# Attention with a two-layer MLP: one chunk's second product is carried from block 1 into block 2

## The chip, the cores and the metric

The kernel runs on one core of a Trainium2 chip. It is one launch, and its time is the device time of that launch in microseconds (us); lower is better. Five instruction streams run side by side on the core: TensorE (PE: matrix products, with the loads of their stationary operand shown as PEld), VectorE (DVE), ScalarE (ACT), GpSimd (POOL), and SyncE (SP), which here only issues transfers. Each takes its instructions in the order in which the program lists them, and they meet at semaphores.

## The reference

Two things are computed one after the other: a linear attention over 8 batches and 8 heads (576 tokens, 64 features per head), and an MLP on the 4608 x 512 result.

```python
q_s = softmax(q, axis=-1)            # over the 64 features of a head
k_s = softmax(k, axis=2)             # over the 576 tokens
kv  = einsum('bhsd,bhse->bhde', k_s, v)
x   = einsum('bhsd,bhde->bhse', q_s, kv)   # then tokens x (heads * 64): 4608 x 512
h   = x @ w_in                       # 512 -> 2048
g   = h * clip(h + 3.0, 0.0, 6.0) / 6.0
out = g @ w_out                      # 2048 -> 512
```

All of it is float32; the weights arrive as float64 words and are decoded in the kernel.

## The kernel before, in words

**Blocks and chunks.** The 4608 tokens are cut into nine blocks of 512 (`j` = 0 to 8), and the 2048 hidden features into 16 chunks of 128 (`f`). For a block and a chunk there is a first product (x with a chunk of `w_in`, into the PSUM tile `ph`), the activation (ACT `L572` and DVE `L573`, giving `g`), a cut of `g` into a coarse and a fine part (`split`: a CAST on ACT at `L123`, a subtraction on DVE at `L124`), and a second product, which adds into four PSUM tiles `po`, one per 128 tokens. Each float32 product is made of three passes (coarse with coarse, coarse with fine, fine with coarse), so a chunk's second product is 12 matmuls of 128x512.

**Two ways of making the first product.** Blocks 0 and 1 use `gemm1`: 12 matmuls of 128x512 for a chunk. From block 2 on, `fast_pair` makes the first product of two chunks at once from seven products of half size (six matmuls of 128x256 each), out of sums of the weights that `fast_weights` has written to DRAM and `fetch` reads back. These seven products go into the tiles x and y (both named `ph`, two buffers) and z (`pz`), and each x has to be copied out by ACT (`L524`, `L530`, `L534`, `L540`) before the next may overwrite it. Between the products stand four gaps, `fill(4)`, `fill(7)`, `fill(7)`, `fill(6)`: so many matmuls of second products that wait in the list `pend` are put there, 24 in all, which is what two chunks have.

**The list `pend`.** `work(j, fs, gs)` is a generator of a chunk's (or a pair's) second-product matmuls; behind the last of a block it calls `store`. In blocks 0 and 1 each iteration makes the first product of chunk `f`, runs what stands in `pend` beyond a limit (`fill_one`), and appends chunk `f`. `store` (lines 596 to 607) scales the four `po` tiles into `ob` tiles, with ACT (`L606`) for tiles 0 and 2 and DVE (`L604`) for tiles 1 and 3, and sends each to DRAM (`L607`). The pool of `ob` has two buffers, taken in turn, and `fast_weights` takes two tiles from the same pool (`s12`, `s34`, `L464`) for sums of weights (`L466` to `L470`), which it then splits (`L468`, `L471`). The four `po` of the next block take the PSUM banks of the four before.

**Order.** From block 1 on the matmuls keep the order in which the code issues them (`keep_in_program_order`); the instructions of the other engines are put in order by a scheduler that works with estimated times and priorities. The attention of a later block (softmax of q and k, `kv`, `px`) is stepped along in between by `slot`, and `fast_weights(7)`, the last pair of weights, is made in the fourth slot of block 2's first pair (line 709).

Of the kernel before, what the change touches and what calls it, by code (L numbers as in the profile page):

```python
# [30 lines left out]
def attention_moe(  # L31
# [33 lines left out]
    NFC = w.shape[0]  # L65
# [60 lines left out]
    def load_w(f, sides=(0, 1)):  # L126
        if f not in raws:
            raws[f] = place(f, U32, f"raw{f}")
        a, b = 2 * DM * sides[0], 2 * DM * (sides[-1] + 1)
        nc.sync.dma_start(  # L130
            raws[f][:, a:b], w[f].rearrange("p s n -> p (s n)")[:, a:b]
        )
# [3 lines left out]
    def decode(f):  # L136

        n = 2 * DM
        pairs = raws.pop(f).rearrange("p (n two) -> p n two", two=2)
        low, high = pairs[:, :, 0], pairs[:, :, 1]
        v = moe.tile([P, n], F32, name="v", bufs=3)
        m = v
        nc.scalar.activation(m, high.bitcast(F32), AF.Abs)  # L148
        nc.vector.tensor_scalar(m, m, W_MIN, W_MAX, op0=ALU.max, op1=ALU.min)
        m = m.bitcast(U32)  # L150
        nc.vector.tensor_scalar(
            m, m, 3, 0x3FFFFFFF, op0=ALU.logical_shift_left, op1=ALU.bitwise_and
        )
        vu = v.bitcast(U32)
        nc.vector.scalar_tensor_tensor(
            vu, high, 0xC0000000, m, op0=ALU.bitwise_and, op1=ALU.bitwise_or
        )
        nc.scalar.activation(low, low, AF.Copy, scale=2.0**-29)
        nc.vector.tensor_tensor(vu, vu, low, op=ALU.add)
        parts = place(f, F32R, f"w_{f}").rearrange("p (s i n) -> p s i n", s=2, i=2)  # L160
        vs = v.rearrange("p (s n) -> p s n", s=2)
        if f not in BY_DMA:
            split(parts[:, :, 0], parts[:, :, 1], vs)
        else:

            hi, lo = parts[:, :, 0], parts[:, :, 1]
            nc.scalar.copy(hi, vs)
            nc.scalar.mul(lo, vs, -1.0)
            nc.gpsimd.dma_start(lo.bitcast(F32), vs, accum_op=ALU.add)
        wi[f], wo[f] = parts[:, 0], parts[:, 1]  # L170
# [280 lines left out]
    def fast_weights(pair):  # L451

        a, b = wi[2 * pair], wi[2 * pair + 1]
        kept[pair] = d = dr.tile([P, 7, 2, HT], F32, name=f"wf{pair}")
        for n, src in ((A11, a[:, :, 0:HT]), (A12, a[:, :, HT:]), (A22, b[:, :, HT:])):
            nc.sync.dma_start(d[:, n], src.bitcast(F32))
        whole = moe.tile([P, 2 * DM], F32, name="m", tag="v", bufs=3)
        for at, src in ((0, a), (TB, b)):
            nc.vector.tensor_add(
                whole[:, at : at + TB], src[:, 0].bitcast(F32), src[:, 1].bitcast(F32)  # L460
            )
        a11, a12, a21, a22 = (whole[:, n * HT : (n + 1) * HT] for n in range(4))
        hi, lo = (t.rearrange("p e n -> p (e n)") for t in (a, b))
        s12, s34 = (moe.tile([P, DM], F32, name="ob", bufs=2) for _ in range(2))  # L464
        s1, s2, s3, s4 = (t[:, n : n + HT] for t in (s12, s34) for n in (0, HT))
        nc.vector.tensor_add(s1, a21, a22)  # L466
        nc.vector.tensor_sub(s2, s1, a11)
        split(hi[:, 0:TB], lo[:, 0:TB], s12)  # L468
        nc.vector.tensor_sub(s3, a11, a21)
        nc.vector.tensor_sub(s4, a12, s2)  # L470
        split(hi[:, TB:], lo[:, TB:], s34)  # L471
        for e, t in enumerate((hi, lo)):
            nc.sync.dma_start(
                d[:, S1 : S4 + 1, e], t.bitcast(F32).rearrange("p (k n) -> p k n", k=4)
            )
# [10 lines left out]
    def fetch(count):  # L486
        for _ in range(count):
            key = next(wanted, None)
            if key is None:
                return  # L490
            j, pair, n = key
            f, h = RING[next(turn) % len(RING)]
            t = wi[f].rearrange("p a n -> p (a n)")[:, h * TB : (h + 1) * TB]
            t = t.rearrange("p (e n) -> p e n", e=2)
            nc.sync.dma_start(t.bitcast(F32), kept[pair][:, ORDER[n][0]])
            come[key] = t
# [65 lines left out]
    def gemm1(j, f):  # L562
        x_hi, x_lo = x_tiles[j]
        ph = ps_h.tile([P, TB], F32, name="ph", tag="ph")
        for cc in range(NCC):
            first, last = cc == 0, cc == NCC - 1
            w_hi, w_lo = (wi[f][:, i, cc * P : (cc + 1) * P] for i in (0, 1))
            mm(ph, w_hi, x_hi[:, cc, :], first, False)
            mm(ph, w_hi, x_lo[:, cc, :], False, False)
            mm(ph, w_lo, x_hi[:, cc, :], False, last)  # L570
        g = moe.tile([P, TB], F32, name="g", bufs=2)
        nc.scalar.activation(g, ph, AF.Relu, bias=three, scale=1.0)  # L572
        nc.vector.scalar_tensor_tensor(g, g, 6.0, ph, op0=ALU.min, op1=ALU.mult)  # L573
        g_hi = moe.tile([P, TB], F32R, name="g_hi", bufs=3)
        g_lo = moe.tile([P, TB], F32R, name="g_lo", bufs=3)
        split(g_hi, g_lo, g)
        return g_hi, g_lo
# [72 lines left out]
    pend = []  # L650
# [6 lines left out]
    def work(j, fs, gs):  # L657

        for f, g in zip(fs, gs):
            for fn, x in gemm2(f, *g, acc(j)):  # L660
                yield fn, x
            if f == NFC - 1:
                store(j, acc(j))
# [10 lines left out]
    def fill_one():  # L674
        for fn, x in pend.pop(0):
            fn(*x)

    for j in range(FAST):
        for f in range(NFC):
            if j == 0:  # L680
                if f + AHEAD < NFC:
                    load_w(f + AHEAD)
            elif not in_order:
                in_order.append(True)
            g = gemm1(j, f)
            if j == 0:
                if f + 2 < NFC:
                    decode(f + 2)
            elif f % 2:
                if f < 15:  # L690
                    fast_weights(f // 2)
                if f >= 7:
                    fetch(1 if f < 15 else 12 - len(come))
            next(step, None)

            while len(pend) > 1 - j:
                fill_one()
            pend.append(work(j, [f], [g]))
    for j in range(FAST, NB):
# [74 lines left out]
```

## Time and profile before

| | |
|---|---|
| median of 3 runs | 886.73 us (885.42 to 887.73) |
| the profiled execution | 889.86 us, span 888.1 us |
| TensorE | busy 855.5 us, 96% of the span |
| VectorE, ScalarE, GpSimd | 616.0, 462.9 and 131.4 us |
| granted TensorE clock, mean | 0.994 |

The span is the profiled stretch from the first to the last instruction; the execution's time has some 1.8 us more around it. A row of the timeline names start and length in us, the engine, the line, the operation, output and inputs, and in brackets how long the engine had been idle and what released it. Nearly all rows of TensorE name line 91, the helper `mm`; they are told apart by their tiles. Block 2's first pair begins at 240.98 us.

### The profile page before, as it was taken

The numbers are of one execution on the slowest core, as the hardware profiler recorded it, in microseconds if no ns is written. First come the engines' busy times: TensorE is split into PE (matmuls) and PEld (weight loads), VectorE is DVE, ScalarE is ACT, GpSimd is POOL, SyncE is SP. The second block draws the span as 40 slices with busy tenths as digits, with TensorE's granted clock in tenths as the row PEclk, the third lists the DMA queues.
The fourth block names the chain that finished last, engine by engine and source line by source line (L and its number), as shares of the span: only waits on it lengthen the run. The fifth ranks groups of instructions, "written<-read, shape, count | busy, mean of one in ns | idle before, by whom it ended". The sixth has DMA issues, their size and how long they took to land.

```text
span 888.1 us, 15250 instructions
## 1 busy us (share of the span) xinstructions
PE 855.5 (96%) x5380; PEld 735.9 (83%) x5380; DVE 616.0 (69%) x1267; ACT 462.9 (52%) x943; POOL 131.4 (15%) x328
## 2 busy tenths in 40 slices
PE   4799999999999999999999999999999999999998
PEld 3477777887788888888888888888888988898896
DVE  7999997899687766767675757675867665434333
ACT  7999644455355454545454545444545554434333
POOL 5000021122112211212020203020212120100000
PEclk9899999999999999999999999999999999999999
DMA  9994653638496767676777677676855575557541
GB/s 368 413 374 136 153 145 109 201 120 275 139 295 203 219 206 244 209 229 199 246 226 221 199 230 248 217 220 188 265 160 175 168 223 169 169 184 214 170 140 47
DMA packets 98202, 184.66 MB, mean 208 GB/s; under 512 B 9808, under 2 KB 24144, under 8 KB 96080
## 3 DMA queue, kind: packets, MB, share of 16 engines
q1 hardware_dynamic: 96192, 180.03, 63.1%
q0 software_dynamic: 1360, 2.62, 1.7%
q10 hardware_dynamic: 576, 1.05, 0.3%
q8 instruction: 43, 0.70, 0.3%
q14 instruction: 31, 0.25, 0.1%
HBM read 156.93 MB, written 24.12 MB: 204 GB/s over the span
## 4 chain that ended last, share of the span: by engine, by line
PE 78%; DMA 5%; DVE 3%; ACT 3%; issue 1%; POOL 0%; SPq 0%; ACTq 0%; POOLq 0%
PE po L91 38%; PE ph L91 30%; PE pz L91 4%; PE px L91 2%; PE pkv L91 2%; DMA qt<-in_qf_dram 2%; DMA out_dram<-ob 1%; DMA w<-v 1%; DMA kt<-in_kT_dram 1%; ACT w L123 0%; DVE w L124 0%; POOL swap L289 0%; PE pm L97 0%; ACT v L434 0%; ACT v L148 0%
## 5 line engine op out<-in xcount | busy, mean ns | idle before, releaser
L91 PE MATMUL po<-w,w 128*128 128x512 f32 x1008 | 261.2, 394 | 2.0 <-ACT w L123 1.9
L91 PEld LDWEIGHTS po<-w,w 128*128 128x128 f32 x1008 | 178.8, 189 | 32.0 <-ACT w L123 2.6
L91 PE MATMUL ph<-x_lo,w 128*128 128x256 f32 (+1 forms) x800 | 151.8, 304 | 1.5 <-DVE x_lo L124 0.6
L91 PEld LDWEIGHTS ph<-w,w 128*128 128x128 f32 x1008 | 134.4, 191 | 11.2 <-DVE second L535 1.6
L91 PE MATMUL ph<-w,w 128*128 128x256 f32 x1008 | 141.1, 285 | 1.4 <-DVE second L535 1.4
L91 PE MATMUL ph<-x_hi,w 128*128 128x256 f32 (+1 forms) x592 | 137.4, 335 | 1.9 <-DVE g L573 1.2
L91 PEld LDWEIGHTS ph<-x_lo,w 128*128 128x128 f32 x800 | 116.3, 189 | 16.5 <-DVE x_lo L124 1.4
L91 PEld LDWEIGHTS ph<-x_hi,w 128*128 128x128 f32 x592 | 92.2, 189 | 16.4 <-DVE x_lo L124 1.8
L124 DVE TENSOR_TENSOR w<-g,w 128x512 fp32r<-128x512 f32 x112 | 77.3, 690 | 36.9 <-ACT w L123 36.9
L123 ACT CAST w<-g 128x512 fp32r<-128x512 f32 x112 | 69.4, 619 | 60.7 <-DVE g L541 37.5
L91 PE MATMUL po<-w 128*128 128x512 f32 x336 | 86.7, 394 | 0.1
L91 PE MATMUL po<-w,g_hi 128*128 128x512 f32 x256 | 67.4, 400 | 1.1 <-ACT g_hi L123 1.1
L91 PEld LDWEIGHTS po<-w 128*128 128x128 f32 x336 | 59.4, 188 | 10.8 <-ACT w L123 0.5
L556 ACT ACTIVATE g<-second,three 128x512 f32<-128x512 f32 x56 | 40.5, 723 | 32.6 <-DVE second L554 26.1
L91 PEld LDWEIGHTS po<-w,g_hi 128*128 128x128 f32 x256 | 46.8, 188 | 11.8 <-ACT g_hi L123 1.6
L540 ACT ACTIVATE g<-ph,three 128x256 f32<-128x256 f32 x56 | 26.6, 474 | 57.2 <-PE ph L91 57.2
L541 DVE SCALAR_TENSOR_TENSOR g<-g,ph 128x256 f32<-128x256 f32 x56 | 23.2, 414 | 47.0 <-ACT g L540 46.8
L534 ACT COPY second<-ph 128x256 f32<-128x256 f32 x56 | 20.8, 372 | 61.9 <-PE ph L91 61.9
L557 DVE SCALAR_TENSOR_TENSOR g<-g,second 128x512 f32<-128x512 f32 x56 | 39.1, 698 | 15.3 <-ACT g L556 15.2
L535 DVE TENSOR_TENSOR second<-second,ph 128x256 f32<-128x256 f32 x56 | 23.2, 414 | 37.3 <-ACT second L534 37.3
L91 PE MATMUL pz<-x_hi,w 128*128 128x256 f32 x336 | 48.9, 281 | 0.0
L289 POOL COPY swap<-qr 32x16 f32<-32x16 f32 x112 | 30.9, 275 | 101.7 <-DVE qr L301 95.1
(125 smaller groups left out, 1258.5 us busy)
## 6 DMA issues: line engine op xcount, KB each, us to landing
w<-wf SPq DMA_DIRECT2D x392, 256.0 KB, 3.2
raw<-in_w_dram SPq DMA_DIRECT2D x16, 1024.0 KB, 13.4
out_dram<-ob SPq DMA_DIRECT2D x36, 256.0 KB, 3.3
vt<-in_v_dram SPq DMA_DIRECT2D x28, 325.0 KB, 3.6
wf<-w SPq DMA_DIRECT2D x16, 512.0 KB, 4.5
kt<-in_kT_dram SPq DMA_DIRECT2D x28, 288.0 KB, 3.0
ke<-in_k_dram SPq DMA_DIRECT2D x24, 320.0 KB, 3.1
qt<-in_qf_dram SPq DMA_DIRECT2D x28, 256.0 KB, 3.3
```

What stands on the lines that cost most here:

```text
L91: nc.tensor.matmul(out, lhsT, rhs, start=start, stop=stop, skip_group_check=goes_on)
L123: nc.scalar.copy(hi, src)
L124: engine.tensor_sub(lo, src, hi.bitcast(F32))
L289: nc.gpsimd.tensor_copy(swap[r : r + QD], stat[o : o + QD])
L534: nc.scalar.copy(second[:, HT:], x)
L535: nc.vector.tensor_add(second[:, HT:], second[:, HT:], y)
L540: nc.scalar.activation(r[:, HT:], x, AF.Relu, bias=three, scale=1.0)
L541: nc.vector.scalar_tensor_tensor(r[:, HT:], r[:, HT:], 6.0, x, op0=ALU.min, op1=ALU.mult)
L556: nc.scalar.activation(r, second, AF.Relu, bias=three, scale=1.0)
L557: nc.vector.scalar_tensor_tensor(r, r, 6.0, second, op0=ALU.min, op1=ALU.mult)
```

## The change

One condition, in the loop over blocks 0 and 1:

```diff
@@ -693,7 +693,7 @@
                     fetch(1 if f < 15 else 12 - len(come))
             next(step, None)
 
-            while len(pend) > 1 - j:
+            while len(pend) > (j == 0 or f == NFC - 1):
                 fill_one()
             pend.append(work(j, [f], [g]))
     for j in range(FAST, NB):
```

In block 0 the limit stays 1, in block 1 it stays 0 but for the last chunk, where it is now 1. So at `f` = 15 of block 1 the second product of chunk 14 is not run; it stays in `pend`, and chunk 15 is appended behind it. Block 2's first pair then has 24 matmuls for its four gaps where it had 12.

**TensorE, where block 1 ends and block 2 begins.** `w_1068` is the place of chunk 14's weights, `w_1135` that of chunk 15's; `pz` and `ph` are products of block 2's first pair. Before:

```order
L91 MATMUL pkv<-vt,ke 64x65 x10
L91 MATMUL po<-w_1068,g_hi 128x512 x8
L91 MATMUL po<-w_1068,g_lo 128x512 x4
L91 MATMUL pz<-x_hi_310,w_588 128x256 x6
L91 MATMUL ph<-x_hi_310,w_588 128x256 x6
L91 MATMUL po<-w_1135,g_hi 128x512 x2
L91 MATMUL po<-w_1135,g_lo 128x512
L91 MATMUL po<-w_1135,g_hi 128x512
L91 MATMUL ph<-w_333,w_657 128x256 x6
L91 MATMUL ph<-w_305,w_657 128x256 x6
L91 MATMUL po<-w_1135,g_hi 128x512
L91 MATMUL po<-w_1135,g_lo 128x512
```

Now:

```order
L91 MATMUL pkv<-vt,ke 64x65 x10
L91 MATMUL pz<-x_hi_310,w_588 128x256 x6
L91 MATMUL ph<-x_hi_310,w_588 128x256 x6
L91 MATMUL po<-w_1068,g_hi 128x512 x4
L91 MATMUL ph<-w_333,w_657 128x256 x6
L91 MATMUL ph<-w_305,w_657 128x256 x6
L91 MATMUL po<-w_1068,g_hi 128x512 x4
L91 MATMUL po<-w_1068,g_lo 128x512 x3
L91 MATMUL px<-qT_hi,kv_hi_0_1445 128x192
L91 MATMUL px<-qT_lo,kv_hi_0_1445 128x192
L91 MATMUL px<-qT_hi,kv_lo_0_1446 128x192
L91 MATMUL px<-qT_hi,kv_hi_0_2311 128x320
```

The 12 matmuls of chunk 14 have left the place ahead of the pair's first product, and the gaps behind the second and the fourth product are filled with them: 4, then 7, with the twelfth and six of chunk 15's in the third gap and chunk 15's last six in the fourth.

**VectorE, the first pair of block 2 and what follows.** With 24 matmuls in `pend` the generator calls `store` only at the `fill()` behind the pair, so it now comes behind `fast_weights(7)` in the code, and its `ob` tiles follow `s12` and `s34` in the pool. Before (`ob_2398` and `ob_2404` take `po` tiles 1 and 3 of block 1, `ob_2463` is `s12`):

```order
L546 SCALAR_TENSOR_TENSOR g_2414<-g_2414,first_2330 128x256
L604 TENSOR_SCALAR ob_2398<-po_1394 128x512
L307 STREAM_TRANSPOSE m_2454<-qt_2427 128x512
L459 TENSOR_TENSOR m_2460<-w_14_1068 128x512
L459 TENSOR_TENSOR m_2460<-w_15_1135 128x512
L604 TENSOR_SCALAR ob_2404<-po_1396 128x512
L124 TENSOR_TENSOR x_hi1_539<-v_2381,x_hi1_539 128x256
L535 TENSOR_TENSOR second_2331<-second_2331,ph_2328 128x256
L124 TENSOR_TENSOR qT_lo_2544<-m_2454,qT_hi_2543 128x512
L466 TENSOR_TENSOR ob_2463<-m_2460 128x256
```

Now there is no `L604` among these; behind `L297` on `qm_3002`, the maximum of the query tile `qt_2996`, come (`ob_2451` is `s12`, `ob_2452` is `s34`, `w_14_1068` and `w_15_1135` take their coarse and fine parts):

```order
L541 SCALAR_TENSOR_TENSOR g_2396<-g_2396,ph_2315 128x256
L467 TENSOR_TENSOR ob_2451<-ob_2451,m_2448 128x256
L124 TENSOR_TENSOR x_lo1_540<-v_2671,x_lo1_540 128x256
L554 TENSOR_TENSOR second_2319<-second_2319,ph_2316 128x256
L470 TENSOR_TENSOR ob_2452<-m_2448,ob_2451 128x256
L290 TENSOR_TENSOR qm_3002<-qm_3002,swap_3005 128x16
L124 TENSOR_TENSOR w_12_958<-g_2396,w_12_958 128x512
L124 TENSOR_TENSOR w_15_1135<-ob_2451,w_14_1068 128x512
L307 STREAM_TRANSPOSE m_2757<-qt_2730 128x512
L299 TENSOR_TENSOR qt_2996<-qt_2996,qm_3002 128x512
L557 SCALAR_TENSOR_TENSOR g_2471<-g_2471,second_2319 128x512
L527 TENSOR_TENSOR first_2491<-first_2491,pz_2490 128x256
```

and directly behind them:

```order
L124 TENSOR_TENSOR w_15_1135<-ob_2452,w_14_1068 128x512
L301 TENSOR_REDUCE qr_3003<-qt_2996 128x16
L124 TENSOR_TENSOR w_13_1017<-g_2471,w_13_1017 128x512
L604 TENSOR_SCALAR ob_2479<-po_1394 128x512
L546 SCALAR_TENSOR_TENSOR g_2570<-g_2570,first_2491 128x256
L297 TENSOR_REDUCE qm_3282<-qt_3276 128x16
L290 TENSOR_TENSOR qr_3003<-qr_3003,swap_3014 128x16
L303 TENSOR_SCALAR qr_3003<-qr_3003 128x16
L304 RECIPROCAL qr_3003<-qr_3003 128x16
L305 TENSOR_TENSOR qt_2996<-qt_2996,qr_3003 128x512
L290 TENSOR_TENSOR qm_3282<-qm_3282,swap_3285 128x16
L604 TENSOR_SCALAR ob_2485<-po_1396 128x512
```

`L604` for `po` tile 1 (`ob_2479`) now stands behind the whole work on the sums of weights, and waits for the last reading of `s34`, whose buffer it takes; `L604` for tile 3 (`ob_2485`) comes eight instructions later and waits until the transfer out of `ob_2479` has ended.

**ScalarE, the same stretch.** Before, both `L606` came ahead of the copy `L434` of `px`, in the first pair:

```order
L123 CAST kv_hi3_0_2311<-kv_2309 128x128
L524 COPY first_2330<-ph_2327 128x256
L606 ACTIVATE ob_2395<-po_1393 128x512
L545 ACTIVATE g_2414<-first_2330,three_90 128x256
L530 COPY second_2331<-ph_2327 128x256
L606 ACTIVATE ob_2401<-po_1395 128x512
L434 COPY v_2381<-px_2374 128x512
```

Now:

```order
L123 CAST w_14_1068<-ob_2452 128x512
L606 ACTIVATE ob_2476<-po_1393 128x512
L300 ACTIVATE qt_2996<-qt_2996 128x512
L123 CAST w_13_1017<-g_2471 128x512
L545 ACTIVATE g_2570<-first_2491,three_90 128x256
L606 ACTIVATE ob_2482<-po_1395 128x512
L300 ACTIVATE qt_3276<-qt_3276 128x512
L530 COPY second_2492<-ph_2488 128x256
L534 COPY second_2492<-ph_2488 128x256
```

`L606` for tile 0 (`ob_2476`) stands behind the cut of `s34`, `L606` for tile 2 (`ob_2482`) behind `L545` of the second pair, and the copies `L530` and `L534` of the second pair come behind `L300` on `qt_3276`, which on VectorE follows `L604` of `ob_2485`. On SyncE the four `L607` now stand among the two writes of the sums of weights (`L473`), and the read of `qt_2996` (`L328`) still follows the fetch (`L495`) that the pair's fifth product releases.

## The prediction

> **What bounds the kernel now.** The page comes first, for its spans, busy shares and the engine shares of the chain of work that ended last.
>
> ```profile
> span 888.1 us, 15250 instructions
> PE 855.5 (96%) x5380; PEld 735.9 (83%) x5380; DVE 616.0 (69%) x1267; ACT 462.9 (52%) x943; POOL 131.4 (15%) x328
> PE 78%; DMA 5%; DVE 3%; ACT 3%; issue 1%; POOL 0%; SPq 0%; ACTq 0%; POOLq 0%
> ```
>
> TensorE is busy 96% of the span and carries 78% of the chain. What the change can win is therefore idle time of TensorE in block 2's first pair, and what it can lose is new idle time there. The timeline of TensorE over the block boundary shows the first:
>
> ```profile
> 237.21 0.95 PE L91 MATMUL pkv<-vt,ke 128*64 128x65 f32 x20
> 238.09 2.13 PE L91 MATMUL po<-w,g_hi 128*128 128x512 f32 x8
> 240.98 0.87 PE L91 MATMUL pz<-x_hi,w 128*128 128x256 f32 x6
> 241.69 0.88 PE L91 MATMUL ph<-x_hi,w 128*128 128x256 f32 x6
> ...
> 246.40 0.25 PE L91 MATMUL px<-qT_hi,kv_hi 128*128 128x192 f32 x1
> ...
> 247.17 0.87 PE L91 MATMUL ph<-x_lo,w 128*128 128x256 f32 x6
> 248.72 0.98 PE L91 MATMUL ph<-x_lo,w 128*128 128x256 f32 x6 [0.44 <-ACT second L534]
> 251.13 0.98 PE L91 MATMUL ph<-w,w 128*128 128x256 f32 x6 [1.43 <-DVE second L535]
> ...
> 253.37 1.09 PE L91 MATMUL po<-w,w 128*128 128x512 f32 x4
> 254.30 1.59 PE L91 MATMUL ph<-w,w 128*128 128x256 f32 x12
> 255.73 1.78 PE L91 MATMUL po<-w,w 128*128 128x512 f32 x7
> 257.35 0.27 PE L97 MATMUL pm<-ident,kb 128*128 128x128 f32 x1
> 257.38 0.97 PE L91 MATMUL ph<-x_lo,w 128*128 128x256 f32 x6
> ```
>
> Two waits, 0.44 and 1.43 us, stand where the third and fourth gap have one matmul and none: the copies of `second` and its sum with y are waited for in the open. Starts, not lengths, give what a matmul costs, since neighbours overlap: six of 128x256 take 0.71 us (240.98 to 241.69), a 128x512 one 0.233 (253.37 to 254.30 for four), the six `px` 0.77 (246.40 to 247.17).
>
> Who is busy behind this? In the 12 us that follow, VectorE is. The table by stretches (columns: stretch, length, then busy us of PE, PEld, DVE, ACT, POOL with counts, granted clock, DMA share, GB/s) and six rows of its timeline:
>
> ```profile
> 252.00:264.00 12.00, 12.00 (x91) 10.52 (x91) 11.40 (x27) 6.77 (x14) 2.98 (x12) 1.00 0.94 307
> 256.31 0.41 DVE L527 TENSOR_TENSOR first<-first,pz 128x256 f32<-128x256 f32 x1
> 256.64 0.69 DVE L124 TENSOR_TENSOR w<-ob,w 128x512 fp32r<-128x512 f32 x1
> 257.24 0.71 DVE L307 STREAM_TRANSPOSE m<-qt 128x512 f32<-128x512 f32 x1
> 257.87 0.72 DVE L299 TENSOR_TENSOR qt<-qt,qm 128x512 f32<-128x512 f32 x1
> 258.51 0.68 DVE L124 TENSOR_TENSOR w<-ob,w 128x512 fp32r<-128x512 f32 x1
> 259.12 0.68 DVE L124 TENSOR_TENSOR w<-g,w 128x512 fp32r<-128x512 f32 x1
> ```
>
> 11.40 of 12 us: a full queue, in which an instruction of 128x512 delays the next by 0.62 us (256.64 to 259.12 for four) and one of 128x256 by 0.33 (256.31 to 256.64).
>
> **The change, part by part. What it wins.** Both orders agree up to 238.09 us. From there the new one puts the products first: `pz` 238.09, product 2 238.80, four `po` 239.51, two products 240.44, seven `po` 241.86, `px` 243.49, product 5 244.26, seven `po` 244.97, product 6 246.60, six `po` 247.31, product 7 248.71, then the second pair's `pz` 249.42 and product 250.13. Its first gap of `po` would start at 250.84, where the trace has 253.37: 2.53 us won, the two waits and the restarts around them. The second product of chunk 14 no longer covers chunk 15's activation, but the four `po` in the first gap need chunk 14's `g` alone, which was ready for 238.09, and the copies of x have seven, seven and six `po` over them (1.6, 1.6 and 1.4 us) against the 0.9 us from a product's start to its copy plus 0.37.
>
> **What it moves: `store`.** The first gap of the second pair needs `po` tiles 0 and 1 empty. Before, they were emptied inside the first pair. Now `L606` and `L604` follow the sums of weights, whose buffers they take. So I walk VectorE's new queue. Its first outside wait is `L297` on the query tile `qt_2996`, whose transfer SyncE issues right behind a fetch that product 5 releases:
>
> ```profile
> 248.07 0.33 SPq L495 DMA_DIRECT2D w<-wf  x1
> 248.49 0.49 SPq L328 DMA_DIRECT2D qt<-in_qf_dram  x1
> qt<-in_qf_dram SPq DMA_DIRECT2D x1, 256.0 KB, 3.6
> qt<-in_qf_dram SPq DMA_DIRECT2D x28, 256.0 KB, 3.3
> ```
>
> The last two rows are the landing of this very transfer and the median of all 28. The fetch went 0.90 us after product 5 began (247.17 to 248.07), the query tile 0.42 later: now 244.26 + 0.90 + 0.42 = 245.58. I take 3.3 us, because fewer transfers stand beside it than at 248.49: it lands at 248.88.
>
> From there the list in the order is nine instructions of 128x512 size up to `L604` of tile 1 (`L297`, `w_12`, `w_15`, `L307`, `L299`, `L557`, `w_15`, `L301`, `w_13`), six of 128x256 and a small one of 0.08: 9 x 0.62 + 6 x 0.33 + 0.08 = 7.64 us, then `L604` itself. Nothing else in the list comes later than its place: ScalarE's casts between them are each released by a VectorE instruction two or more places earlier.
>
> ```profile
> 243.30 0.60 ACT L606 ACTIVATE ob<-po 128x512 f32<-128x512 f32 x1 [0.32 <-PE po L91]
> 249.72 0.69 DVE L604 TENSOR_SCALAR ob<-po 128x512 f32<-128x512 f32 x1 [1.80 <-PE ph L91]
> 258.65 0.64 ACT L300 ACTIVATE qt<-qt 128x512 f32<-128x512 f32 x1
> 253.93 0.35 ACT L524 COPY first<-ph 128x256 f32<-128x256 f32 x1
> DMA to landing us min/median/max: 2.0/3.3/4.8
> ```
>
> - Tile 0: `L606` waits for the first `w_15`: `L297`, five short ones, the small one, `w_12` and `w_15` itself end at 248.88 + 0.62 + 1.65 + 0.08 + 0.62 + 0.69 = 252.54; plus 0.60 for `L606` and 0.05 to restart TensorE: 253.19. TensorE waits from 250.84, **2.35 us**, and runs two `po` (to 253.66).
> - Tile 1: `L604` ends at 248.88 + 7.64 + 0.69 = 257.21. TensorE restarts at 257.26, a wait of **3.60 us**. Two `po`, two products and two `po` of tile 2 (its `L606` waits for the store of tile 0, issued some 3.5 us before tile 1's, and is done by then) bring it to 257.26 + 0.47 + 1.42 + 0.47 = 259.62.
> - Tile 3: its `ob` is tile 1's, so the store of tile 1 has to land: 257.24 + 3.3 (the last row is the landing of all `out_dram` transfers) = 260.54, `L604` 0.69: 261.23, restart 261.28, a wait of **1.66 us**. Five `po`: 262.44.
> - The next product needs the copy `L530`, now behind `L300` of `qt_3276`, behind `L299`, behind that `L604`: 261.23 + 0.62 + 0.64 + 0.35 (the row of `L524`, a copy of the same size) = 262.84, **0.40 us** more.
>
> This product stands at 257.38 in the trace: the kernel is then 262.84 - 257.38 = **5.46 us late** (the waits add to 8.01, less 2.53). TensorE is busy 12.00 of the 12 us from 252, and its next wait in the trace is that of the next boundary, so nothing is there in which this could be caught up, and it is carried to the end.
>
> SyncE's queue changes too. The fetches behind the store of tile 3 wait with it until 261, some 2 us past the products that release them. I cost that at nothing: each refills one of twelve weight buffers, so eleven others are used first, over a pair's length (240.98 to 252 and more); without this cover it would be those 2 us again. The two `L473` are read six pairs later.
>
> **The clock.** The one large wait that the trace has behind a store is at the next boundary. The rows are ScalarE's, TensorE's and two stretches of the table:
>
> ```profile
> 346.47 0.60 ACT L606 ACTIVATE ob<-po 128x512 f32<-128x512 f32 x1 [3.76 <-DMA out_dram<-ob]
> 347.62 1.20 PE L91 MATMUL po<-w,w 128*128 128x512 f32 x4 [1.92 <-ACT w L123]
> 350.89 2.49 PE L91 MATMUL po<-w,w 128*128 128x512 f32 x7
> 353.22 0.27 PE L97 MATMUL pm<-ident,kb 128*128 128x128 f32 x1
> 349.00:352.00 3.00, 3.00 (x14) 2.81 (x13) 2.62 (x5) 1.43 (x4) 0.00 (x0) 0.50 0.73 219
> 247.50:251.20 3.70, 1.83 (x13) 1.30 (x11) 1.90 (x5) 2.13 (x5) 0.00 (x0) 1.00 0.90 288
> ```
>
> After 1.92 us of idleness the clock fell to 0.50, and `po`, two products and `po` took 353.22 - 347.62 = 5.60 us where the pair at 253.37 took 3.98: 1.62 us lost. The waits at 248 to 251 did not do that (clock 1.00). The new waits are longer, so I expect a fall, but most of the slow stretch (some 3 us) should lie under the waits for tiles 1 and 3. Bounds 0 and 1.62; I take 0.4, a quarter, as most of it is covered.
>
> The Trainium skill (TensorE: Matmul & The Clock Gate, Part 1 and "Why this matters for your kernels") asks for no idle gap of over about 3 us and lets the clock halve after an idle window of about 3.4 us. This trace is stricter, since 1.92 us sufficed; by the skill only the wait of 3.60 us would count, and, as an estimate, one window at half rate would add up to 1.7 us where none of it is covered.
>
> **Sum.** -2.53 + 2.35 + 3.60 + 1.66 + 0.40 + 0.4 = **+5.9 us**. On the profiled execution (889.86 us, span 888.1) this is 895.8 and a span of 894.0. That execution is 3.1 us above the median of the runs, 886.73; the difference carries over, so **892.6 us**.
>
> Its bounds: the two transfers on the path, the query tile and the store of tile 1, at 2.0 us each come 1.3 us earlier each: 2.9 late with no clock term, 889.6 us. At 4.8 us each they come 1.5 later each: 8.5, and with the whole 1.62 of the clock 10.1, 896.8.
>
> **Rivals.**
> 1. *The stores are not late (not slower).* If `L606` and `L604` ended by 250.8 and 251.3, the gaps would be won and nothing paid: -2.5, 884.2 us. For it: later blocks fill all four gaps as this one now would, and the row below gives 2.0 us of idleness ahead of all their 1008 `po` matmuls of this form. Against it: this boundary alone has `fast_weights` between, and tile 1 would have to be out 5.9 us earlier than its place in VectorE's list allows. Chance 0.06.
>
> ```profile
> L91 PE MATMUL po<-w,w 128*128 128x512 f32 x1008 | 261.2, 394 | 2.0 <-ACT w L123 1.9
> ```
>
> 2. *Only tile 0 is late.* TensorE goes on at 253.19 against 253.37, the same within 0.2 us, 886.5 us; it decides if `L604` of tile 1 is over by 253.6, which would need VectorE's list to be 3.6 us shorter. Chance 0.10.
> 3. *The waits feed each other.* Slow transfers (4.8 us) and a clock that stays at half speed into the part without waits: +8 to +10, 894.7 to 896.8, or beyond if the fall repeats. For it: the boundary at 346.47, where a store was waited for 3.76 us. Chance 0.14.
>
> That the change does not do what it says is excluded by TensorE's order.
>
> **Chances.** The forecast has 0.70. The range 887.5 to 896.5 us runs from just above rival 2 over most of rival 3; rivals 1 and 2 and the end of 3, some 0.2, are left out. A measurement of this kernel tells about 0.3%, 2.7 us, from no change. Rival 1's 2.5 us is just below that, so faster has 0.04; the same 0.12 (rival 2 and the rest of 1); slower 0.84.
>
> **What would show it.** In the new profile: TensorE's two waits in the first pair gone and its `pz` of the second pair near 249.4; then three idle rows before `po`, released by ACT `L606`, DVE `L604`, DVE `L604`, of about 2.4, 3.6 and 1.7 us; `L297` waiting for the query tile near 248.9; a stretch at clock 0.5 between 253 and 262. Wrong would be: no idle row named `ob` before 262 us, or `L604` of tile 1 before 254 us. If the waits are there but the time is unchanged, the end does not hang on this boundary, and my reading of the chain is wrong.

## The result, and the profile after

The changed kernel takes 893.25 us (median of 13 runs, 889.85 to 895.25), the kernel before 887.73 us (13 runs, 885.42 to 891.78). The ratio is 1.0057, with a 95% interval of 1.0045 to 1.0069: slower by 0.6%, 5.5 us by the medians.

The page of the changed kernel, its spans, its busy shares and the largest group of second products of blocks 2 to 8, 1008 of them (busy us, mean ns of one, idle us just before them and what ended most of it):

```profile
span 892.9 us, 15249 instructions
PE 859.1 (96%) x5380; PEld 740.1 (83%) x5380; DVE 617.1 (69%) x1267; ACT 463.7 (52%) x943; POOL 132.1 (15%) x328
L91 PE MATMUL po<-w,w 128*128 128x512 f32 x1008 | 262.3, 395 | 6.9 <-DVE ob L604 3.2
```

The shares say nothing: TensorE is at 96% as before. The group says where to look. Its idle time went from 2.0 to 6.9 us, and what ends it is now `ob`, the store, where it was the cut `w`. TensorE's timeline over the boundary shows the place:

```profile
239.07 0.95 PE L91 MATMUL pkv<-vt,ke 128*64 128x65 f32 x20
...
250.69 0.87 PE L91 MATMUL ph<-w,w 128*128 128x256 f32 x6
251.40 0.87 PE L91 MATMUL pz<-x_hi,w 128*128 128x256 f32 x6
252.10 0.87 PE L91 MATMUL ph<-x_hi,w 128*128 128x256 f32 x6
255.03 0.73 PE L91 MATMUL po<-w,w 128*128 128x512 f32 x2 [2.05 <-ACT ob L606]
258.92 1.22 PE L91 MATMUL po<-w,w 128*128 128x512 f32 x2 [3.16 <-DVE ob L604]
259.94 2.76 PE L91 MATMUL ph<-w,w 128*128 128x256 f32 x12
262.50 2.65 PE L91 MATMUL po<-w,w 128*128 128x512 f32 x7
265.00 0.27 PE L97 MATMUL pm<-ident,kb 128*128 128x128 f32 x1
265.02 0.97 PE L91 MATMUL ph<-x_lo,w 128*128 128x256 f32 x6
...
354.78 1.20 PE L91 MATMUL po<-w,w 128*128 128x512 f32 x4 [1.55 <-ACT w L123]
```

Between `pkv` and the second pair no row has a bracket: the waits of 0.44 and 1.43 us are gone. In their place stand 2.05 and 3.16 us, for `po` tiles 0 and 1. Behind them no idle row comes before 354.78, but the rows themselves are long: seven `po` took 2.50 us (262.50 to 265.00), where the kernel before needed 1.62. The table by stretches tells why (the last three columns are granted clock, DMA share, GB/s):

```profile
256.00:257.00 1.00, 0.00 (x0) 0.00 (x0) 1.00 (x4) 1.00 (x3) 0.00 (x0) 1.00 1.00 293
257.00:258.00 1.00, 0.00 (x0) 0.00 (x0) 1.00 (x3) 0.20 (x1) 0.27 (x1) 0.79 0.80 248
258.00:259.00 1.00, 0.08 (x1) 0.08 (x1) 1.00 (x3) 0.00 (x0) 0.88 (x4) 0.50 1.01 381
...
263.00:264.00 1.00, 1.00 (x4) 0.81 (x3) 0.30 (x2) 0.89 (x2) 0.00 (x0) 0.50 0.87 309
264.00:265.00 1.00, 1.00 (x5) 0.73 (x5) 0.44 (x1) 0.00 (x0) 0.38 (x2) 0.80 0.93 246
265.00:266.00 1.00, 1.00 (x9) 1.00 (x8) 0.44 (x3) 0.00 (x0) 0.69 (x3) 1.00 0.45 162
```

From 257.6 to 264.4 the granted clock is 0.50. And VectorE's timeline shows why the stores came when they did:

```profile
250.70 0.69 DVE L297 TENSOR_REDUCE qm<-qt 128x16 f32<-128x512 f32 x1 [0.51 <-DMA qt<-in_qf_dram]
...
253.66 0.68 DVE L124 TENSOR_TENSOR w<-ob,w 128x512 fp32r<-128x512 f32 x1
...
256.39 0.68 DVE L124 TENSOR_TENSOR w<-ob,w 128x512 fp32r<-128x512 f32 x1
257.00 0.68 DVE L301 TENSOR_REDUCE qr<-qt 128x16 f32<-128x512 f32 x1
257.59 0.68 DVE L124 TENSOR_TENSOR w<-g,w 128x512 fp32r<-128x512 f32 x1
258.19 0.68 DVE L604 TENSOR_SCALAR ob<-po 128x512 f32<-128x512 f32 x1
...
261.76 0.69 DVE L604 TENSOR_SCALAR ob<-po 128x512 f32<-128x512 f32 x1 [0.16 <-DMA out_dram<-ob]
```

After a short wait for the query tile (0.51 us) it works without a pause through the list, both cuts of the sums of weights (`w<-ob,w`) among it, and reaches `L604` of tile 1 at 258.19.

Where the 4.8 us between the two spans lie (892.9 against 888.1): the changed execution reaches the boundary 1.86 us later (`pkv` at 239.07 against 237.21), where the programs are still alike; from this `pkv`, ahead of block 2's first pair, to the next one, in its second pair, it takes 30.57 us against 24.76, **5.81 us more**; from there to the transpose `pm` in block 3's second pair it takes 2.04 less, since its wait at that boundary was 1.55 us and the clock stayed up, against 1.92 us and a fall in the profile before; the rest is 0.83 less. Only the 5.81 us lie where the change is; the other three are of the size by which executions of one program differ (the runs of the kernel before spread over 6 us). In the experiments I therefore read the time from `pkv` to the next `pkv` beside the medians.

### The profile page after: what moved, and what is told of

It is laid out like the page before. It is cut to its first block, busy times and chain, and to the rows that moved or that the text cites. A ratio compares the mean times of both kernels' runs of the same rounds, so it can differ in the third digit from the quotient of the medians.

```text
span 892.9 us, 15249 instructions
## 1 busy us (share of the span) xinstructions
PE 859.1 (96%) x5380; PEld 740.1 (83%) x5380; DVE 617.1 (69%) x1267; ACT 463.7 (52%) x943; POOL 132.1 (15%) x328
## 4 chain that ended last, share of the span: by engine, by line
PE 78%; DMA 5%; DVE 3%; ACT 3%; issue 1%; POOL 0%; ACTq 0%; DVEq 0%; POOLq 0%
PE po L91 38%; PE ph L91 30%; PE pz L91 4%; PE px L91 2%; PE pkv L91 2%; DMA qt<-in_qf_dram 2%; DMA w<-v 1%; DMA kt<-in_kT_dram 1%; DMA out_dram<-ob 1%; DVE w L124 1%; ACT w L123 0%; ACT ob L606 0%; POOL swap L289 0%; DVE qt L299 0%; PE pm L97 0%
## 5 line engine op out<-in xcount | busy, mean ns | idle before, releaser
L534 ACT COPY second<-ph 128x256 f32<-128x256 f32 x56 | 20.8, 372 | 63.1 <-PE ph L91 63.1
L535 DVE TENSOR_TENSOR second<-second,ph 128x256 f32<-128x256 f32 x56 | 23.2, 413 | 37.2 <-ACT second L534 37.2
```

The source lines that it names most:

```text
L534: nc.scalar.copy(second[:, HT:], x)
L535: nc.vector.tensor_add(second[:, HT:], second[:, HT:], y)
```

## The experiments

The theory, A: the stores are late because their tiles follow `s12` and `s34` in a pool of two buffers; take this away and the time goes below the kernel before. Its rival, B: moving the second product costs the time in itself, whatever the stores do.

**The sums in buffers of their own.** The last pair's `s12` and `s34` take a buffer each of `g_hi` and `g_lo`, which have three; all else is the changed kernel.

```diff
-        s12, s34 = (moe.tile([P, DM], F32, name="ob", bufs=2) for _ in range(2))
+        if pair < NFC // 2 - 1:
+            s12, s34 = (moe.tile([P, DM], F32, name="ob", bufs=2) for _ in range(2))
+        else:
+            s12 = moe.tile([P, DM], F32, name="s12", tag="g_hi", bufs=3)
+            s34 = moe.tile([P, DM], F32, name="s34", tag="g_lo", bufs=3)
```

> The changed kernel, with the last pair's sums of weights (s12, s34) in spare buffers of g_hi and g_lo, so that the stores of block 1 no longer wait for them; the matmul order stays that of the change. Theory A (the loss comes from the stores standing behind the sums of weights in the shared pool): the waits for po tiles 0, 1 and 3 go; left is about 0.5 us before the second pair's first gap, where the cast of g stands behind the store copy of tile 2, which waits for tile 0's transfer. The second pair's fifth product comes about 1.9 us earlier than in the kernel before, 7.7 us earlier than in the changed one: some 885.5 to 887 us where the kernel before has 887.7. Rival B (the moved second product itself costs the time, since it no longer covers the end of block 1): nothing changes, about 893 us.

885.69 us against 886.91 for the kernel before (29 runs on the chip of this and the next three experiments), ratio 0.9981 (0.9962 to 0.9999). TensorE's timeline of this kernel, from the second pair's first products on:

```profile
249.95 0.87 PE L91 MATMUL pz<-x_hi,w 128*128 128x256 f32 x6
250.66 0.87 PE L91 MATMUL ph<-x_hi,w 128*128 128x256 f32 x6
251.42 1.20 PE L91 MATMUL po<-w,w 128*128 128x512 f32 x4
...
263.07 0.98 PE L91 MATMUL ph<-x_hi,w 128*128 128x256 f32 x6 [0.17 <-DVE g L545]
...
266.04 1.70 PE L91 MATMUL ph<-w,w 128*128 128x256 f32 x12 [1.07 <-DVE second L558]
```

The four `po` follow the product at once; both `ob` rows are gone. From `pkv` to the next `pkv` it takes 22.70 us, 2.06 less than before, near the 2.53 us that the prediction gave the filled gaps (a run further down shows that not all of it is theirs). But 1.24 us of it come back in the third pair, as waits for VectorE. The medians show 1.2 us.

**The store ahead of the sums.** A `fill()` before the call of `fast_weights(7)` runs the pair's list to its end there, so that `store` comes first in the code.

```diff
                 if j == FAST and not pair and done[0] == 4:
+                    fill()
                     fast_weights(NFC // 2 - 1)
```

> The changed kernel, with store(1) called in the fourth slot ahead of fast_weights(7), by emptying the finished list there; matmul order and buffers are those of the change, only who takes the two ob buffers first is turned round. Theory A: as with own buffers, about 1.9 us faster than the kernel before (885.5 to 887 us); the sums of weights now wait for the stores' transfers, which nothing needs soon. Rival B: about 893 us.

886.55 us, ratio 1.0005 (0.9986 to 1.0023). At the boundary it does the same as the kernel above: 22.53 us from `pkv` to `pkv`, 2.23 less than before, no `ob` row. Then 0.18, 0.48 and 0.43 us of waits stand in the third pair and after. The loss is gone, but the 1.9 us expected below before did not show in the time.

**Late stores without the carried product.** The kernel before, with its own order of products, but with `store` of block 1 moved behind `fast_weights(7)`:

```diff
-            if f == NFC - 1:
+            if f == NFC - 1 and j != 1:
                 store(j, acc(j))
 ...
                     fast_weights(NFC // 2 - 1)
+                    store(1, acc(1))
```

> The kernel before with its matmul order, and store(1) moved behind fast_weights(7): the one side effect of the change without the change. Theory A: the three waits for po tiles stand there, the two filled gaps do not, so it is slower than the kernel before by about 7.7 us and slower than the changed one by about 2: 894 to 897 us. Rival B: like the kernel before, 887.7 us.

894.1 us (6 runs), ratio 1.007 (1.0047 to 1.0093), and 32.06 us from `pkv` to `pkv`, 7.30 more than before. Its TensorE, where the second pair's first gap begins:

```profile
257.83 1.22 PE L91 MATMUL po<-w,w 128*128 128x512 f32 x2 [4.00 <-ACT ob L606]
260.54 1.22 PE L91 MATMUL po<-w,w 128*128 128x512 f32 x2 [1.49 <-DVE ob L604]
```

The wait for tile 3 has no row here either. Nothing is carried, and the loss is there in full, larger by 1.49 us than in the changed kernel, whose gaps are filled. This decides against B: the late store alone makes the kernel slow, and the carried product without it does not.

**One of the two buffers.** The changed kernel with `s34` alone in a buffer of its own:

```diff
-        s12, s34 = (moe.tile([P, DM], F32, name="ob", bufs=2) for _ in range(2))
+        s12 = moe.tile([P, DM], F32, name="ob", bufs=2)
+        if pair < NFC // 2 - 1:
+            s34 = moe.tile([P, DM], F32, name="ob", bufs=2)
+        else:
+            s34 = moe.tile([P, DM], F32, name="s34", tag="g_lo", bufs=3)
```

> The changed kernel with only s34 in a spare buffer; s12 still takes an ob buffer, so one link of the chain is taken out: tile 0 is free at once, tile 1 waits for tile 0's transfer, tile 2 for the first use of s12, tile 3 for tile 1's transfer behind the rest of VectorE's list. Theory A, from the changed kernel's rows: no wait for tile 0 and 1 beyond 0.3 us, about 0.6 us for tile 2 and 1.9 us for tile 3, together 2.5 to 2.8 us, which is what the filled gaps win: within 1 us of the kernel before, 887 to 889 us. Rival B: about 893 us.

888.44 us, ratio 1.0014 (0.9995 to 1.0032): between the two, as A has it. Its TensorE at the second pair's second gap (`L610` and `L608` are the store, moved down by the added lines):

```profile
253.00 0.73 PE L91 MATMUL po<-w,w 128*128 128x512 f32 x2 [0.20 <-ACT ob L610]
255.95 1.64 PE L91 MATMUL po<-w,w 128*128 128x512 f32 x5 [2.22 <-DVE ob L608]
```

The waits are 0.20 and 2.22 us; the clock fell behind the second, and `pkv` to `pkv` is 26.87 us, 2.11 more than before.

**The last two tiles apart.** The question was whether the prediction's third and fourth wait (tile 3, and the copy behind it), which have no idle row in the profile after, were paid for. Tiles 2 and 3 of block 1's store take buffers of `g_hi` and `g_lo`:

```diff
-            if j < NB - 1:
+            if j == 1 and t > 1:
+                tag = ("g_hi", "g_lo")[t % 2]
+                ob = moe.tile([P, DM], F32, name="ob", tag=tag, bufs=3)
+            elif j < NB - 1:
```

> The changed kernel with tiles 2 and 3 of block 1's store in buffers of their own (those of g_hi and g_lo); tiles 0 and 1 still take the buffers of s12 and s34. Theory A (the prediction's third and fourth wait, 1.66 us for tile 3 behind the store of tile 1 and 0.40 us for the copy behind it, are paid for): both go, and the time is 2.06 us below the changed kernel, 3.5 to 4 us above before. Rival B (they are paid for by nobody, since the clock at half speed after the first two waits makes the products ahead of tile 3 last long enough to cover them): the two idle rows for tiles 0 and 1 stay at 2 and 3 us, the granted clock still falls to 0.50 behind them, and the time is that of the changed kernel within 0.5 us, 5 to 6 us above before.

889.45 us against 887.58, ratio 1.002 (1.0004 to 1.0036): neither expectation holds. Measured against the kernel before it is 3.7 us better than the changed kernel, more than A gave, and TensorE's timeline shows that the edit did something else besides:

```profile
252.49 1.09 PE L91 MATMUL po<-w,w 128*128 128x512 f32 x4
253.42 1.60 PE L91 MATMUL ph<-w,w 128*128 128x256 f32 x12
255.19 0.73 PE L91 MATMUL po<-w,w 128*128 128x512 f32 x2 [0.18 <-ACT ob L609]
258.82 2.50 PE L91 MATMUL po<-w,w 128*128 128x512 f32 x5 [2.90 <-DVE ob L607]
```

The first gap runs all its four `po` without a wait. Tiles 2 and 3 are now emptied first, and block 2's first two `po` get the PSUM banks that came free first; in the program they no longer wait for tiles 0 and 1, and its third and fourth `po` do. So the late stores of tiles 0 and 1 are met in the second gap, half a pair later, and cost 0.18 + 2.90 us there instead of 2.05 + 3.16. What tile 3 alone cost is not told apart by this run.

**The way out, in four steps on one chip.** Two edits take away what a store waits for. In the first, `fast_weights(7)` is made in block 1's chunk 15, so that it is out of the pool before the store. In the second, tiles 2 and 3 of the stores of blocks 1 to 7 take buffers of `g_hi` and `g_lo`, so that no boundary has a store waiting for another ("four places").

```diff
# fast_weights(7) in chunk 15
-                if f < 15:
-                    fast_weights(f // 2)
+                fast_weights(f // 2)
 ...
-                if j == FAST and not pair and done[0] == 4:
-                    fast_weights(NFC // 2 - 1)
# four places
-            if j < NB - 1:
+            if 0 < j < NB - 1 and t > 1:
+                tag = ("g_hi", "g_lo")[t % 2]
+                ob = moe.tile([P, DM], F32, name="ob", tag=tag, bufs=3)
+            elif j < NB - 1:
```

The changed kernel with the first edit:

> The changed kernel with the last pair's sums of weights (fast_weights(7)) made one place earlier, in block 1's chunk 15, and no longer in block 2's first pair. Theory A (the stores are late because their tiles follow s12 and s34): the stores are early again, so the 5.8 us of the changed kernel go, and the 1.9 us that the kernel with tiles of their own was ahead of the kernel before are kept. What is new: some 4.5 us of VectorE work leave the first two pairs, where that kernel gave back 1.07 + 0.17 us in the third pair; if that backlog was the sums, these waits go and the time is 2 to 3 us below before (884 to 885); if it was not, about 1.9 below (885). Rival B (the work moved to chunk 15 makes chunk 15's activation late, by its two additions of 128x256 and a cut, 1.2 us and more): before or up to 1.5 us above it (887 to 888.5), with an idle row of TensorE ahead of block 2's first pair or its first gaps.

The kernel with the store ahead of the sums (the `fill()` above), with the second edit:

> The changed kernel with the stores ahead of fast_weights(7) in the code, and, for blocks 1 to 7, with tiles 2 and 3 of a store in two other buffers (those of g_hi and g_lo), so that no store waits for a store. Theory A (what is lost at a block's boundary is the store waiting for buffers): TensorE has no idle row before po at the boundary of blocks 1 and 2, which is worth the 1.9 us that the same kernel without the four places showed, and none at the boundary of blocks 2 and 3, where the profiles lost between 0 and 3.7 us by execution (1.6 in the changed kernel, 3.7 in the one before): 883 to 885 us, 2 to 4 below before. Rival B (the wait at the boundary of blocks 2 and 3 stems from VectorE's full queue, not from the buffers): that wait stays, and the time is that of the kernel without the four places, 885 to 887.

The kernel before, with the second edit, without the carried product:

> The kernel before, so without the carried second product, with the same four places for the stores of blocks 1 to 7. Its first pair of block 2 keeps the two waits of 0.44 and 1.43 us. Theory A: it gains at the boundary of blocks 2 and 3 alone, 0 to 3.5 us: 884 to 887, and stands 1.5 to 2.5 us above the kernel with both, which is then the worth of the filled gaps by themselves. Rival B (filled gaps are worth nothing, since VectorE's backlog hands the waits on to the next pairs): no difference between the two.

The changed kernel with both edits:

> The changed kernel with fast_weights(7) in block 1's chunk 15 and the four places. Theory A: both gains together, no idle row before po at either boundary and no backlog on VectorE in the third pair: 882 to 884.5 us, 2.5 to 5 below before and not above the kernel with the four places and fast_weights(7) in the first pair. Rival B (the earlier sums hold up chunk 15's activation): 0.5 to 1.5 us above that kernel.

The kernel before had 887.91 us on this chip (35 runs). "Boundary" is from the `pkv` ahead of block 2's first pair to the one in its second, "to block 3" from there to the transpose `pm` in block 3's second pair; the kernel before has 24.76 and 91.25 us.

| kernel | median, us | ratio (95%) | boundary | to block 3 |
|---|---|---|---|---|
| changed, sums in chunk 15 | 886.30 | 0.9988 (0.9970 to 1.0005) | 23.14 | 89.38 |
| changed, store first, four places | 884.70 | 0.9973 (0.9960 to 0.9985) | 22.47 | 88.09 |
| before, four places | 885.96 | 0.9992 (0.9979 to 1.0005) | 24.08 | 87.43 |
| changed, sums in chunk 15, four places | 883.68 | 0.9967 (0.9950 to 0.9985) | 22.35 | 87.41 |

The second and fourth are faster than both kernels of this case. From each other they can't be told: the means of their 12 runs differ by 0.6 us, give or take 1.4 (95%). The group of second products shows for the second:

```profile
L91 PE MATMUL po<-w,w 128*128 128x512 f32 x1008 | 260.1, 393 | 0.0
```

These 1008 `po` of blocks 2 to 8 wait for nothing, and the second kernel's time is what theory A gave. But a boundary of blocks 2 and 3 without an idle row does not by itself show what the four places do: the profiles with the sums in buffers of their own, with the store first and with one of the two buffers have none there either, without the places. What differs is ScalarE's `L606` for tile 2 at that boundary. In the three profiles with the places it waits 0.22 us, for TensorE. In six of the eight without them it waits for a store's transfer: 3.38 to 3.76 us in four, where TensorE then lost 1.53 to 1.92 us, and 1.71 and 1.76 us in two, where it lost nothing. The four places alone, on the kernel before, show 1.9 us by the medians, but the interval of their ratio still holds 1.

Between the second and the third row lies the carried product with its filled gaps (and the `fill()` that keeps the store first): the means of the runs differ by 1.7 us, give or take 0.9, and the boundaries by 1.61. So the change is worth something, as soon as the store does not pay for it.

It is worth less than the 2.1 to 2.4 us by which these boundaries are shorter than that of the kernel before. The third kernel was expected to keep both, 0.44 and 1.43 us, since its gaps are as empty; it keeps only the first:

```profile
249.17 0.98 PE L91 MATMUL ph<-x_lo,w 128*128 128x256 f32 x6 [0.44 <-ACT second L534]
250.18 0.98 PE L91 MATMUL ph<-w,w 128*128 128x256 f32 x6
252.32 0.98 PE L91 MATMUL ph<-x_hi,w 128*128 128x256 f32 x6 [0.46 <-DVE g L541]
```

The sum `L535`, for which TensorE waited 1.43 us, stands on VectorE two places behind `L604` of tile 3. In the kernel before, VectorE idled 1.80 us ahead of this `L604` (the row at 249.72 in the prediction); with a buffer of its own for the tile it idles 0.40 us, and both come 1.4 us earlier after `pkv`. So most of the 1.43 us was a store in front of the sum. That the store waited there for the transfer of tile 1 fits the edit that ended it, but is inferred: the profile names a product of TensorE, which `L604` does not read. The filled gaps by themselves are worth 1.61 us at the boundary with the stores out of the way on both sides, and 1.49 us with both stores late (30.57 against 32.06).

The first row's expectation held for the boundary (1.62 us below before) and for the waits in the third pair, which are gone, not for the time: 1.6 us by the medians, with 1 inside the interval. Its profile has a wait at the next boundary,

```profile
346.89 1.20 PE L91 MATMUL po<-w,w 128*128 128x512 f32 x4 [1.72 <-ACT w L123]
```

which is absent in the fourth row. The kernel before waits there too (1.92 us), so this does not explain why no more was won. The rival there, that earlier sums hold up chunk 15's activation, has one row for it, in the profile of the fourth kernel, ahead of chunk 13's second product:

```profile
232.79 2.12 PE L91 MATMUL po<-w,g_hi 128*128 128x512 f32 x8 [1.31 <-ACT g_hi L123]
```

The second kernel has no idle row there, but the same row has 0.72 us in the profile before, and 0.36 in that of the first kernel, whose sums are as early. The medians give the rival no support, though by the means half a microsecond of it is not excluded. Whether the waits in the third pair (1.07 and 0.17 us above) came from the sums is open too: they are absent where the sums are in chunk 15, but nearly absent (0.18) in the second kernel and absent in the third, which have them in the first pair.

## Why the prediction was right, and what was mis-sized

The forecast was 892.6 us (887.5 to 896.5), slower with 0.84; 893.25 was measured. The forecast difference was +5.9 us, the measured one 5.5; that the times agree to 0.65 us owes something to luck, since the median of the kernel before came out 1.0 us higher than the 886.73 us that the forecast started from. Since the two executions reach the boundary at other times, each step is compared by its distance from `pkv` at the boundary:

| step | before | predicted | measured |
|---|---|---|---|
| second pair begins (`pz`) | 14.74 | 12.21 | 12.33 |
| query tile there, `L297` starts | | 11.67 | 11.63 |
| `po` of tile 0 starts | 16.16 | 15.98 | 15.96 |
| `po` of tile 1 starts | | 20.05 | 19.85 |
| `L604` of tile 3 starts | | 23.33 | 22.69 |
| fifth product of the second pair | 20.17 | 25.63, with the clock 26.03 | 25.95 |

- **The gaps filled, -2.53 us.** Measured: the second pair's first gap would have begun at 13.74 (its product at 252.10 plus 0.71) against 16.16, -2.42. The size held, the reason only in part: the prediction put both waits down to the empty gaps, but most of the 1.43 us was `L604` of tile 3 in front of the sum on VectorE, which the change moved out of the way together with the store. By the experiments the filled gaps alone are worth 1.5 to 1.6 us.
- **Tile 0, 2.35 us, and tile 1, 3.60 us.** From the end of the work ahead to the restarts: 15.96 - 13.74 = 2.22, and 19.85 - 15.96 - 0.47 = 3.42. The brackets say 2.05 and 3.16, because the modelled end of a row of matmuls lies 0.16 to 0.26 us behind the normal start of the next (0.87 against 0.71, 0.73 against 0.47). The two steps they rest on held: the query tile took 3.1 us from its issue (247.57 in the rows below) to `L297` at 250.70, where 3.3 was put in, and VectorE's list from `L297` to `L604` took 258.19 - 250.70 = 7.49 us against 7.64. That the place of an instruction in a full queue, counted in steps of 0.62 and 0.33 us, gives its time to 0.15 us is what carried these two terms. The rows of SyncE's queue and of ScalarE in the changed kernel on which these and the next readings rest:

```profile
247.57 0.37 SPq L328 DMA_DIRECT2D qt<-in_qf_dram  x1
...
258.90 1.76 SPq L607 DMA_DIRECT2D out_dram<-ob  x2
```

```profile
263.09 0.63 ACT L300 ACTIVATE qt<-qt 128x512 f32<-128x512 f32 x1 [2.79 <-DVE qt L299]
263.62 0.35 ACT L530 COPY second<-ph 128x256 f32<-128x256 f32 x1
```

- **Tile 3, 1.66 us; the copy `L530`, 0.40; the clock, 0.4.** Here the sum is right and its parts are not what the profile shows. From the restart for tile 1 to the fifth product 6.10 us were measured, where 5.58 + 0.4 was forecast; at full clock and without any wait it is 3.52 us of work. No bracket names tile 3 or the copy. The store of tile 1, issued at 258.90, had landed by 261.76, 2.9 us later, and `L604` of tile 3 ended at 262.45. The twelve matmuls of the two products ahead took 2.56 us instead of 1.42, and the first two of the seven `po` some 0.93 (2 x 0.233 at half speed), so that tile 3 was not needed before 263.4. `L530` ended at 263.97, a microsecond before the fifth product. The clock term was mis-sized: TensorE worked some 5.5 us at half speed (258.92 to 264.40), an estimated 2.7 us lost, most of it where the two waits would have been. At full speed tile 3 would have been needed at 261.28 (258.92 + 0.47 + 1.42 + 0.47), 1.2 us ahead of its `L604`, against the forecast 1.66, and the copy would have held up the fifth product by 0.35 us more, against 0.40. So by these rows the two waits come to 1.6 us where 2.06 was forecast, and the clock adds 1.0 us to them where 0.4 was forecast. That the sum of the three held (2.58 us measured, 2.46 forecast) is in part luck: the errors cancel. No run shows the waits without the slow clock, since the one meant for it changed the order of the banks.
- **SyncE's fetches at nothing.** Held: there is no idle row of TensorE from 258.92 to 354.78.
- **Carried to the end.** Held in the median (5.5 us against the 5.8 of the boundary). In the pair of profiles 2.04 us of it are hidden by the next boundary, which was dearer in the profile before than in any of the others: 91.25 us, where all the runs listed here have 87.4 to 90.0.
- **The rivals.** Stores not late, and only tile 0 late, fell with the rows for both tiles; the experiments brought about the first by edits (no wait for a store, 885.69 and 886.55 us), and for the second something like it: one long wait of 2.22 us, though not for tile 0 (888.44 us). Of the third rival one half came true: the clock stayed at half speed into the part without waits, for two stretches. The other half did not, the transfers took 3.1 and 2.9 us, so the total stayed at the forecast.

## What to carry to other kernels

When a change lets one more piece of work wait in a list, look at what stands behind the list's end, here a store, and which pool its tiles come from: the turn of a pool is fixed by the order in the code, and a tile taken one call later can stand behind unrelated work that took a tile before it. The time of such a late instruction can be had beforehand by counting the steps in front of it in its engine's queue from the last outside event. Buffers are the cheap cure: two places out of other pools, and one call moved, turned a loss of 5.5 us into a gain of 3 to 4 by the medians. And a wait that stands where a gap is empty need not be the gap's: look at what stands in front of its releaser in that engine's queue.

## What the runs showed of the hardware

**The clock falls for a fixed stretch.** Two rows of 0.2 us each, of the kernel before, at both ends of its fall:

```profile
349.00:349.20 0.20, 0.20 (x4) 0.20 (x3) 0.20 (x1) 0.20 (x1) 0.00 (x0) 0.54 0.34 102
352.40:352.60 0.20, 0.20 (x2) 0.16 (x2) 0.20 (x1) 0.03 (x1) 0.00 (x0) 0.93 1.07 410
```

and of the changed one:

```profile
257.40:257.60 0.20, 0.00 (x0) 0.00 (x0) 0.20 (x2) 0.00 (x0) 0.00 (x0) 0.94 0.55 199
...
264.20:264.40 0.20, 0.20 (x2) 0.19 (x1) 0.20 (x1) 0.00 (x0) 0.00 (x0) 0.50 0.95 236
264.40:264.60 0.20, 0.20 (x3) 0.16 (x2) 0.04 (x1) 0.00 (x0) 0.03 (x1) 1.00 0.72 174
```

All between them are at 0.50. A mean of 0.54 over 0.2 us means that the fall began 0.016 us into it; so worked out, the stretches are 349.02 to 352.43, 3.41 us, and 257.58 to 264.40, 6.82 us, twice that. The same came out in the late store without the carried product (257.76 to 264.58, 6.83), with one of the two buffers (256.98 to 260.40, 3.42) and with the last two tiles apart (258.34 to 261.75, 3.41). I had taken "some 3 us" and thought of one fall for all the waits; in the changed kernel it was two stretches. The Trainium skill (TensorE: Matmul & The Clock Gate, "What's actually happening") gives a free-running window of 4096 cycles, 3413 ns, and the trace agrees with this length.

**What sets it off is less than an idle window.** In the 3.41 us ahead of a fall TensorE need not be idle all the time: by the rows shown it worked 1.49 us of them in the kernel before (one wait of 1.92 us), and 0.73 us in the changed one, whose second slow stretch followed one in which it had worked 2.07 of 3.41 us. Waits of 1.72, 1.55, 1.53 and 1.20 us, each alone, were followed by no fall. The Trainium skill's rule of no gap above about 3 us (TensorE: Matmul & The Clock Gate, "Why this matters for your kernels") would have allowed the waits of 1.92, 2.22 and 2.90 us; the clock fell behind the first two and within the third. For this kernel a wait near 2 us has to be taken as one that may cost up to an estimated 1.7 us more, half a stretch of 3.41 us.

**PSUM banks went to the next block in the order in which they were emptied.** That is a matter of the program and not of the chip, and one run shows it: the edit that was to free tiles 2 and 3 alone also moved the waits for tiles 0 and 1 to a later gap.
